# A gated linear recurrence feeding a top-1 expert layer: experts processed in the rank of their counts, with room by rank and shared tiles in quarters

## The chip, the cores and the metric

The kernel runs on one core of one Trainium2 chip. A core has a matrix engine (TensorE, shown as PE for the matmuls and PEld for its loads of the stationary operand), a vector engine (DVE), a scalar engine (ACT), GpSimd (POOL) and SyncE (SP), which here only issues DMAs. All engines run their own instruction streams in order and wait for each other through semaphores. 16 DMA engines move data between HBM and the on-chip memory (SBUF); matmuls write to PSUM, which has eight banks. The metric is the device time of one execution in microseconds.

## The reference

```python
# attention: B, H, S, D = 4, 8, 768, 48
mag = sqrt(a_re**2 + a_im**2); scale = minimum(mag, 0.999) / (mag + 1e-6)
a_re, a_im = a_re * scale, a_im * scale
for t in range(S):                       # complex state (D x D) per batch and head
    new_re = ar * S_re - ai * S_im
    new_im = ar * S_im + ai * S_re
    S_re, S_im = new_re + outer(k[t], v[t]), new_im
    y[t] = q[t] @ S_re
x = y as (3072 tokens, 384)              # B*S tokens, H*D columns
# expert layer: 8 experts, hidden size 1024
logits = x @ w_gate                      # (3072, 8)
e = argmax(logits); gate = softmax(logits)[e]
out[token] = gate * (relu(x[token] @ w1[e]) @ w2[e])     # w1: 384x1024, w2: 1024x384
```

Each token goes to exactly one expert, so how many tokens an expert gets depends on the data. With the given inputs the reference sends 354, 406, 392, 388, 370, 421, 338 and 403 tokens to experts 0 to 7.

## The kernel before

The kernel has two stages, and each has an order of instructions that is written out ahead of time. A class `Plan` collects operations with an engine, an assumed duration, what they read and write, and for DMAs an assumed latency and time on the wire. `Plan.order` tries many list schedules with slightly different priorities (seeded noise) and keeps the one with the shortest planned span; the instructions are then emitted in that order, so every engine's stream is the planner's choice. Changing one operation's assumed duration can change the order of all the others.

**Stage one (plan P)** computes the recurrence by chunks of 128 tokens. `front(u)` turns the gates of one unit (up to 384 tokens of one batch) into scaled q and k with ACT, DVE and POOL and moves them by DMA (`hz<-zp`) into a layout for matmuls. `chunk(b, c)` does the matmuls of one chunk: scores (L403), masking on DVE (`am`), outputs (L415, L422), the state (L430), and at the end L438, which turns the result so that tokens lie on partitions and adds the eight logits; ACT copies it into `xg`.

`route(b, r0, r1)` handles several chunks at a time: maximum, softmax sum, one-hot choice, and a place for each token. The place comes from matmuls with a strictly triangular matrix and a matrix of ones (L479 to L484) plus `cumb`, the running counts, which start at `e * CAP`: expert `e` owns rows `e * CAP` to `e * CAP + CAP - 1` of the HBM tensor `xs_hbm`, with `CAP = 448`. POOL then scatters each chunk's 128 rows with one indirect DMA (L498). Each row holds the token's features, its gate weight and its token number. Places from 256 on that no token takes are filled beforehand by three DMAs of 64 rows for each expert from the tile `empty` (L531), with a token number that is out of bounds, so that nothing is written for them later. Batches 0 to 2 are routed once; batch 3 is routed in three parts, chunks 0 to 2, 3 to 4 and 5.

**Between the stages** a few DVE operations and two matmuls (L560, L570) check that the fast way is valid, among other things that every expert's count lies between 256 and `CAP`. If not, the flag `again` sends the program into a slow loop that recomputes everything.

**Stage two (plan M)** processes experts 0 to 7 in order. `weights(e)` loads w1 (L611) and w2 (L613) of expert `e`, 1.5 MB each, into one of three buffers; for experts 0 and 1 that happens before anything else of the plan. `tokens(e, s)` fetches the expert's 448 rows with four DMAs (`xb<-xs_hbm`, L620; for expert 0 two of the four go through the ACT queue), and the gate weights and token numbers (`gi`, `hg`). DVE transposes the rows in 32x32 blocks (L632) into `xrt`. Then:

- L647, first product: 8 hidden parts of 128 by 3 steps over the features, each a matmul with 448 moving columns. DVE (L650) and ACT (L653) take turns at the relu into `ht`.
- L661, second product: for the first 384 tokens, three output tiles of 128 tokens; each is 8 matmuls with 384 moving columns (the w2 columns), the tokens being the stationary operand.
- L673, shared tiles: the remaining 64 places of two neighbouring experts share one output tile, one expert at partitions 0 to 63, the other at 64 to 127. Each of the 8 steps is two matmuls with 64 stationary columns and 384 moving columns.
- `finish`: DVE multiplies with the gate weight into one of four `yo` buffers (L605), and POOL scatters the 128 rows to the output by token number (L594).

All matmuls here are fp32, and each shows as two MATMUL records in the trace, with a LDWEIGHTS record each. So 24 matmuls of one expert's first product are 48 records.

Of the kernel before, what the change touches and what calls it, by code (L numbers as in the profile page):

```python
# [30 lines left out]
CAP = 448  # L31
# [3 lines left out]
NB = CAP // 32  # L35
# [129 lines left out]
def gateloop_then_moe(ctx, tc, gates, qk, v, wg, w1, w2, out):  # L165
# [50 lines left out]
    ones_b = const([128, 128], "ones_b", 1.0, BF16)  # L216
    cum = const([128, E], "cum")
# [7 lines left out]
    with ExitStack() as att:  # L225
# [278 lines left out]

        def setup():
# [14 lines left out]
        with tc.manual_schedule():  # L520
            for u in range(NU):
# [7 lines left out]
                if u == 3:  # L529
                    for h in range(3):  # L530
                        P.add("SP", 0.65, lambda h=h: nc.sync.dma_start(  # L531
                            xs_hbm.rearrange("(e s) w -> s e w", e=E)[MINC + 64 * h:MINC + 64 * h + 64],
                            bc(empty[0:64, None, :], [64, E, W])), (), (("empty", h),), lat=2, wire=3.2, after=moved[1])
                for c in range(t0 // 128, t1 // 128):
                    chunk(b, c, t1 - t0 == TU)
                    for r0, r1 in ROUTES[b]:
                        if r1 == c + 1:
                            route(b, r0, r1)
            for i in P.order():
# [25 lines left out]
    nc.vector.tensor_scalar(out=f4, in0=f4, scalar1=float(CAP), scalar2=None, op0=ALU.is_le)  # L565
# [8 lines left out]
    with ExitStack() as ms:  # L574
# [4 lines left out]
        NW = 3  # L579
        w1b = buf("w1b", NW, [128, DT * F])  # L580
        w2b = buf("w2b", NW, [128, FT * DM])
        xrt = buf("xrt", 2, [128, DT, CAP])
        ht = buf("ht", 2, [128, FT, CAP])
        yo = buf("yo", 4, [128, DM])
        hg = buf("hg", 2, [128, 2])
        xb = buf("xb", 2, [128, NB, 96])
        gi = buf("gi", 2, [128, 3, 2])
        HB, OB = bank[0:5], bank[5:8]
        M = Plan()
# [12 lines left out]
        def finish(ob, gate, index, reads):  # L602
            yi = cnt["y"] % 4
# [5 lines left out]
        def weights(e):  # L609
            ws = e % NW  # L610
            M.add("SP", 0.65, lambda: nc.sync.dma_start(w1b[ws], w1[e * 128:e * 128 + 128, :]), (), (("w1", ws),), lat=1.9, wire=5.2,  # L611
                  after=rows[-1:])
            M.add("SP", 0.65, lambda: nc.sync.dma_start(w2b[ws], w2[e * 128:e * 128 + 128, :]), (), (("w2", ws),), lat=1.9, wire=5.2,  # L613
                  after=rows[-1:])

        def tokens(e, s):

            for i in range(4):
                eng, dma = ("ACT", nc.scalar) if e == 0 and i % 2 else ("SP", nc.sync)
                j = M.add(eng, 0.65, lambda i=i, dma=dma: dma.dma_start(  # L620
                    xb[s][32 * i:32 * i + 32], xs_hbm[e * CAP:(e + 1) * CAP, 104 * i:104 * i + 96].rearrange("(j p) w -> p j w", p=32)),
                    ("routed",), (("xb", s, i),), lat=2.5 if e == 0 else 6.0, wire=0.9)
            if e:
                rows.append(j)
            z, hgi = e % 2, e // 2 % 2
            M.add("SP", 0.65, lambda: nc.sync.dma_start(
                gi[s], xs_hbm[e * CAP:e * CAP + 384, XW:W].rearrange("(j p) w -> p j w", p=128)), ("routed",), (("gi", s),), lat=3.0, wire=0.5)
            M.add("SP", 0.65, lambda: nc.sync.dma_start(
                hg[hgi][64 * z:64 * z + 64], xs_hbm[e * CAP + 384:(e + 1) * CAP, XW:W]), ("routed",), (("hg", hgi, z),), lat=3.0, wire=0.1)
            for j in range(4):  # L630
                b0, b1 = 4 * j, min(4 * j + 4, NB)
                M.add("DVE", (b1 - b0) * 96 * 0.00105 + 0.1, lambda b0=b0, b1=b1: nc.vector.transpose(  # L632
                    xrt[s][:, :, 32 * b0:32 * b1].rearrange("p d (b t) -> p b d t", t=32),
                    xb[s][:, b0:b1].rearrange("p b (d c) -> p b d c", d=DT)), tuple(("xb", s, i) for i in range(4)), (("xrt", s, j),))

        def expert(e):
            s, ws = e % 2, e % NW
            if e > 1:
                weights(e)
            tokens(e, s)  # L640
# [204 lines left out]
```

## Time and profile before

| | |
|---|---|
| median of 6 runs | 565.81 us (564.5 to 569.49) |
| the profiled execution | 566.71 us, of which 565.0 us are its span |
| mean granted TensorE clock | 0.934 |
| busy in the span | PE 479.2, PEld 322.7, DVE 269.2, ACT 201.6, POOL 112.0 us |
| stage one ends with the matmuls of the check | 257.73 us |
| first matmul of stage two | 267.22 us |
| last shared tile starts | 554.53 us |
| first product, 384 records | 150.9 us busy |
| second product, 384 records | 128.4 us busy |
| shared tiles, 128 records | 21.5 us busy |

A record's own duration is longer than its share of the time, because matmuls overlap in the pipeline: what a matmul costs in a row of them is the distance from one start to the next. The numbers of lines are those of the kernel before.

### The profile page before, as it was taken

Reading aid. Unit: us, or ns where it says so; the run is one execution under the profiler, and the core shown is the slowest. Engines: PE = TensorE matmul, PEld = TensorE weight load, DVE = VectorE, ACT = ScalarE, POOL = GpSimd, SP = SyncE. Lnnn points to the kernel's source line nnn. Section 1 sums busy time; section 2 is a strip of 40 time slices with the busy share of each in tenths; the row PEclk is TensorE's granted clock in tenths of the full one; section 3 lists DMA queues with packets and bytes.
Section 4 is the critical chain, followed back from the end, with each engine's and each line's share of the span. In section 5 each row is a group of like instructions: output and inputs, shape, how many; then the busy total and the mean of one; then the engine's idle time right before and its main releaser. Section 6 shows DMA issues by size and latency. Waiting matters only on the chain. (4 is left out here: it accounts for less than half of the span.)

```text
span 565.0 us, 6970 instructions
## 1 busy us (share of the span) xinstructions
PE 479.2 (85%) x2689; PEld 322.7 (57%) x2689; DVE 269.2 (48%) x429; ACT 201.6 (36%) x289; POOL 112.0 (20%) x116
## 2 busy tenths in 40 slices
PE   0065797976988999971999999999999999999996
PEld 0055696865877989860455545555455554555552
DVE  6899989798999997333212021022011120110111
ACT  6896788888687676220100000100000000000100
POOL 6253113044512510430001001010011010100202
PEclk9996779696998899995899999999999999999999
DMA  8767666659999873876926063067343300400101
GB/s 266 206 209 201 162 215 177 203 155 293 289 243 224 258 177 106 329 293 119 280 37 174 15 172 139 13 237 181 52 149 127 112 29 0 139 14 0 34 24 48
DMA packets 48425, 86.15 MB, mean 152 GB/s; under 512 B 22513, under 2 KB 37905, under 8 KB 46337
## 3 DMA queue, kind: packets, MB, share of 16 engines
q1 hardware_dynamic: 43840, 75.19, 47.2%
q0 software_dynamic: 3328, 9.86, 4.7%
q10 hardware_dynamic: 1216, 0.59, 0.5%
q8 instruction: 23, 0.38, 0.3%
q14 instruction: 18, 0.14, 0.1%
HBM read 54.32 MB, written 13.21 MB: 120 GB/s over the span
## 5 line engine op out<-in xcount | busy, mean ns | idle before, releaser
L647 PE MATMUL bank<-xrt,w1b 128*128 128x448 f32 x384 | 150.9, 546 | 9.3 <-DVE xrt L632 9.3
L661 PE MATMUL bank<-w2b,ht 128*128 128x384 f32 x384 | 128.4, 487 | 0.0
L647 PEld LDWEIGHTS bank<-xrt,w1b 128*128 128x128 f32 x384 | 74.0, 193 | 79.2 <-issue 63.4
L653 ACT ACTIVATE ht<-bank 128x448 f32<-128x448 f32 x32 | 17.4, 544 | 254.6 <-PE bank L647 229.6
L661 PEld LDWEIGHTS bank<-w2b,ht 128*128 128x128 f32 x384 | 72.7, 190 | 54.3 <-issue 10.3
L403 PE MATMUL bank<-hz 128*128 128x128 f32 x384 | 61.4, 313 | 36.4 <-DMA hz<-zp 35.4
L403 PEld LDWEIGHTS bank<-hz 128*128 128x128 f32 x384 | 54.6, 221 | 40.4 <-issue 32.6
L594 POOL DMA_INDIRECT out_dram<-yo,gi x24 | 23.5, 980 | 271.1 <-DVE yo L605 245.8
L650 DVE TENSOR_SCALAR ht<-bank 128x448 f32<-128x448 f32 x32 | 20.0, 624 | 95.2 <-PE bank L647 90.9
L605 DVE TENSOR_SCALAR yo<-bank,gi 128x384 f32<-128x384 f32 x24 | 14.8, 617 | 96.6 <-PE bank L661 91.8
L422 PE MATMUL bank<-am,v 128*48 128x128 f32 x384 | 30.3, 292 | 19.9 <-DVE am L178 19.6
L178 DVE TENSOR_TENSOR zp<-Z,cs 128x1152 f32<-128x1152 f32 (+2 forms) x40 | 44.5, 1151 | 3.6 <-ACT cs L267 1.5
L178 POOL TENSOR_TENSOR AB<-AB,C 128x1152 f32<-128x1152 f32 (+2 forms) x9 | 22.3, 2478 | 81.7 <-ACT C L267 81.7
L498 POOL DMA_INDIRECT xs_hbm<-xg,slot x24 | 26.8, 1115 | 51.0 <-issue 16.0
L438 PE MATMUL bank<-turn,yt 128*128 128x104 f32 x192 | 30.7, 308 | 7.1 <-ACT yt L426 5.6
L322 DVE TENSOR_TENSOR_SCAN D<-AB,lend,C 128x384 f32<-128x384 f32 (+2 forms) x30 | 36.6, 1269 | 0.3
L422 PEld LDWEIGHTS bank<-am,v 128*48 128x48 f32 x384 | 20.9, 129 | 24.7 <-DVE am L178 22.4
L178 DVE TENSOR_TENSOR am<-bank,causal 128x512 f32<-128x512 f32 x48 | 31.7, 678 | 5.5 <-PE bank L403 5.5
L430 PE MATMUL bank<-v,kt 128*96 128x48 f32 x320 | 33.9, 263 | 0.3 <-ACT kt L398 0.3
L430 PEld LDWEIGHTS bank<-v,kt 128*96 128x96 f32 x320 | 32.3, 181 | 2.7 <-issue 1.7
L632 DVE STREAM_TRANSPOSE xrt<-xb 128x384 f32<-128x384 f32 (+1 forms) x32 | 14.0, 496 | 40.0 <-PE bank L647 32.6
L438 PEld LDWEIGHTS bank<-turn,yt 128*128 128x128 f32 x192 | 27.1, 216 | 9.2 <-ACT yt L426 6.1
(110 smaller groups left out, 477.8 us busy)
## 6 DMA issues: line engine op xcount, KB each, us to landing
w1b<-in_w_dram SPq DMA_DIRECT2D x8, 1536.0 KB
w2b<-in_w_dram SPq DMA_DIRECT2D x8, 1536.0 KB
hz<-zp SPq DMA_DIRECT2D x24, 432.0 KB
AB<-in_gates_dram SPq DMA_DIRECT2D x12, 576.0 KB
Z<-in_qk_dram SPq DMA_DIRECT2D x12, 576.0 KB
xb<-xs_hbm SPq DMA_DIRECT2D x30, 168.0 KB
v<-in_v_dram SPq DMA_DIRECT2D x8, 576.0 KB
xs_hbm<-empty SPq DMA_DIRECT2D x3, 836.0 KB
```

The costliest lines, as they stand in the source:

```text
L178: (eng or nc.vector).tensor_tensor(out=o, in0=a, in1=b, op=op)
L322: P.add("DVE", 2 * T * 0.00105 + 0.19, lambda g=g: nc.vector.tensor_tensor_scan(d[:, g, :], a[:, g, :], c[:, g, :], lend[:, b, g, c0:c0 + ...
L403: nc.tensor.matmul(SC[hf][:, (h % 4) * 128:(h % 4) * 128 + 128], lhsT=hk[:, h], rhs=hq[:, h], start=True, stop=True)
L422: nc.tensor.matmul(YT[ps, (h // 2) * 128:(h // 2) * 128 + 128], lhsT=V[:, cl, h * D:h * D + D], rhs=am[2 * par + hf][:, h % 4, :], start=( ...
L430: nc.tensor.matmul(ST[0:96, h * D:h * D + D], lhsT=kt[par][:, h * 96:h * 96 + 96], rhs=V[:, cl, h * D:h * D + D], start=(c == 0 and h == 0 ...
L438: nc.tensor.matmul(XT[:, p * 104:p * 104 + 104], lhsT=yt[par][:, p * 128:p * 128 + 128], rhs=turn[:, p, :], start=True, stop=True)
L498: i = nc.gpsimd.indirect_dma_start(out=xs_hbm[:, :], out_offset=bass.IndirectOffsetOnAxis(ap=R[slot][:, c:c + 1], axis=0), in_=xg[:, (g0 + ...
L594: i = nc.gpsimd.indirect_dma_start(out=out[:, :], out_offset=bass.IndirectOffsetOnAxis(ap=index, axis=0), in_=y, in_offset=None, bounds_ch ...
L647: nc.tensor.matmul(HB[hb][:, 0:CAP], lhsT=w1b[ws][:, c:c + 128], rhs=xrt[s][:, d, :], start=(d == 0), stop=(d == DT - 1))
L650: M.add("DVE", 0.6, lambda f_=f_, hb=hb: nc.vector.tensor_scalar_max(ht[s][:, f_, :], HB[hb][:, 0:CAP], 0.0), (("H", hb),), (("ht", s, f_),))
L653: M.add("ACT", 0.6, lambda f_=f_, hb=hb: nc.scalar.activation(ht[s][:, f_, :], HB[hb][:, 0:CAP], func=ACT.Relu), (("H", hb),), (("ht", s, ...
L661: nc.tensor.matmul(OB[ob][:, 0:DM], lhsT=ht[s][:, f_, j * 128:j * 128 + 128], rhs=w2b[ws][:, f_ * DM:f_ * DM + DM], start=(f_ == 0), stop= ...
```

## The change

1. **Room by rank.** `CAP` becomes 480 places in HBM for each expert, but the number of places that are computed depends on the rank of the expert's count: `CAPS`. The ranks are found on the chip by `ranks()`, from the counts after 21 of the 24 chunks (after the route of chunks 0 to 2 of batch 3): one matmul and six small DVE operations write `order`, the expert of each rank.
2. **Order of experts by rank.** Stage two runs over turns 0 to 7; turn `e` takes the expert of rank `TURNS[e]`. Its number is read into a register on SP (for turn 0 on ACT as well), and weights, rows, gate weights and token numbers are fetched from addresses that the register gives. All of these loads now have to wait for `order`. Only the weights of turn 0 are ahead of the first rows; before, it was two experts' weights.
3. **Shared tiles by 32.** Three experts share one output tile in quarters of 32 rows, twice: places 384 to 479 of turn 0 and 384 to 415 of turn 1 in one tile, places 384 to 447 of turn 2 and 384 to 415 of turns 3 and 4 in another. Turns 5 to 7 have 384 places and no rest. To keep what they need, there are four w2 buffers and three `ht` buffers instead of three and two.
4. **Fill** of the places from 256 on in parts of 64, 64 and 96 rows for each expert, instead of three times 64.
5. **Eight output buffers** `yo` instead of four.
6. **The check** compares the final counts, taken by rank, with `CAPS`.

```diff
-CAP = 448
+CAP = 480
+CAPS = (480, 448, 416, 416, 416, 384, 384, 384)
+TURNS = (0, 2, 1, 3, 4, 5, 6, 7)
+SHARED = ((1, ((0, 384, 0), (0, 416, 32), (0, 448, 64), (1, 384, 96))), (4, ((2, 384, 0), (2, 416, 32), (3, 384, 64), (4, 384, 96))))
...
+        def ranks():
+            cnt = bank[2][:, 440:440 + E]
+            P.add("PE", 0.3, lambda: nc.tensor.matmul(cnt, lhsT=ones_b, rhs=cumb, start=True, stop=True), ("cumb",), ("RT",))
+            def dv(fn, r, w):
+                P.add("DVE", 0.2, fn, r, w)
+            full = [128, E, E]
+            dv(lambda: tt(key, cnt, keyb, ALU.subtract), ("RT",), ("key",))
+            dv(lambda: tt(tmp, bc(key[:, None, :], full), bc(key[:, :, None], full), ALU.is_le), ("key",), ("tmp",))
+            dv(lambda: nc.vector.tensor_reduce(above, tmp, axis=AX, op=ALU.add), ("tmp",), ("above",))
+            dv(lambda: tt(pick, bc(above[:, None, :], full), bc(rev[:, :, None], full), ALU.is_equal), ("above",), ("pick",))
+            dv(lambda: tt(tmp, pick, bc(e_f[:, None, :], full), ALU.mult), ("pick", "above"), ("tmp",))
+            def f():
+                    nc.vector.tensor_reduce(order, tmp, axis=AX, op=ALU.add)
+            dv(f, ("tmp",), ("order",))
+            P.add("", 14.0, lambda: None, ("order",), ("prefetch",))
...
                     for h in range(3):
-                            xs_hbm.rearrange("(e s) w -> s e w", e=E)[MINC + 64 * h:MINC + 64 * h + 64],
-                            bc(empty[0:64, None, :], [64, E, W])), (), (("empty", h),), lat=2, wire=3.2, after=moved[1])
+                        h0, h1 = MINC + 64 * h, (MINC + 64, MINC + 128, CAP)[h]
+                            xs_hbm.rearrange("(e s) w -> s e w", e=E)[h0:h1],
+                            bc(empty[0:h1 - h0, None, :], [h1 - h0, E, W])), (), (("empty", h),), lat=2, wire=3.7, after=moved[1])
...
                         if r1 == c + 1:
                             route(b, r0, r1)
+                            if b == B - 1 and r1 == 3:
+                                ranks()
...
-    nc.vector.tensor_scalar(out=f4, in0=f4, scalar1=float(CAP), scalar2=None, op0=ALU.is_le)
+    tt(tmp, pick, bc(f4[:, None, :], [128, E, E]), ALU.mult)
+    nc.vector.tensor_reduce(f4, tmp, axis=AX, op=ALU.add)
+    tt(f4, f4, caps, ALU.is_le)
...
-        NW = 3
+        NW, NV, NH = 3, 4, 3
-        w2b = buf("w2b", NW, [128, FT * DM])
+        w2b = buf("w2b", NV, [128, FT * DM])
-        ht = buf("ht", 2, [128, FT, CAP])
-        yo = buf("yo", 4, [128, DM])
+        ht = buf("ht", NH, [128, FT, CAP])
+        yo = buf("yo", 8, [128, DM])
...
         def weights(e):
+            def f():
+                which[e] = ds(nc.values_load(order[0:1, TURNS[e]:TURNS[e] + 1], engines=ENG[0:2 if e == 0 else 1], min_val=0, max_val=E - 1,
+                                             skip_runtime_bounds_check_because="experts have numbers below E"), 1)
+            M.add("SP", 0.3, f, (), (("which", e),), after=rows[-1:])
+            for wb, wv, nb, nm in ((w1b, w1v, NW, "w1"), (w2b, w2v, NV, "w2")):
+                first = M.add("SP", 0.65, lambda wb=wb, wv=wv, nb=nb: nc.sync.dma_start(wb[e % nb][:, None, :], wv[:, which[e], :]),
+                              (("which", e),), ((nm, e % nb),), lat=1.9, wire=5.2, after=rows[-1:] if nm == "w1" else [first])
...
-                    xb[s][32 * i:32 * i + 32], xs_hbm[e * CAP:(e + 1) * CAP, 104 * i:104 * i + 96].rearrange("(j p) w -> p j w", p=32)),
+                    xb[s][32 * i:32 * i + 32, None, 0:nb, :], xv[:, which[e], 0:nb, 104 * i:104 * i + 96]),
...
-                        nc.tensor.matmul(HB[hb][:, 0:CAP], lhsT=w1b[ws][:, c:c + 128], rhs=xrt[s][:, d, :], start=(d == 0), stop=(d == DT - 1))
+                        nc.tensor.matmul(HB[hb][:, 0:n], lhsT=w1b[e % NW][:, c:c + 128], rhs=xrt[s][:, d, 0:n], start=(d == 0), stop=(d == DT - 1))
...
-                        for z in range(2):
-                            nc.tensor.matmul(OB[ob][64 * z:64 * z + 64, 0:DM], lhsT=ht[z][:, f_, 384:CAP],
-                                             rhs=w2b[(e - 1 + z) % NW][:, f_ * DM:f_ * DM + DM], start=(f_ == 0), stop=(f_ == FT - 1),
-                                             skip_group_check=True)
+                            for t, m, c0, p0 in parts:
+                                nc.tensor.matmul(OB[ob][p0:p0 + m, 0:DM], lhsT=ht[t % NH][:, f_, c0:c0 + m],
+                                                 rhs=w2b[t % NV][:, f_ * DM:f_ * DM + DM], start=(f_ == 0), stop=(f_ == FT - 1),
+                                                 skip_group_check=len(parts) > 1)
...
             weights(0)
-            weights(1)
```

## The prediction

> **What bounds the kernel now.** I read the chain of what ended last first; it holds only four pieces, the last 1.1 us, so it does not say what sets the span. Next the page's slices of 14.1 us:
>
> ```profile
> PE   0065797976988999971999999999999999999996
> DVE  6899989798999997333212021022011120110111
> PEclk9996779696998899995899999999999999999999
> ```
>
> DVE leads up to slice 15, then come a few slices of mixed work, one slice in which PE is nearly empty, and from there PE alone. The windows put numbers on it (the columns are the stretch, its length, the busy time of PE, PEld, DVE, ACT and POOL, PE's clock, the DMA share and GB/s):
>
> ```profile
> 120.00:180.00 60.00, 50.35 (x519) 45.06 (x518) 58.03 (x70) 47.41 (x68) 21.25 (x14) 0.91 0.94 250
> 225.00:258.00 33.00, 24.38 (x267) 21.51 (x265) 11.35 (x58) 8.30 (x19) 12.40 (x15) 0.90 0.70 271
> 258.00:267.00 9.00, 0.00 (x0) 0.00 (x0) 1.69 (x5) 0.00 (x0) 0.01 (x1) 0.50 0.74 150
> 333.00:360.00 27.00, 27.00 (x94) 13.57 (x93) 3.73 (x6) 1.63 (x3) 1.96 (x2) 1.00 0.34 97
> 450.00:500.00 50.00, 50.00 (x162) 26.60 (x161) 8.64 (x16) 2.18 (x4) 4.89 (x5) 1.00 0.15 54
> ```
>
> From 267 us PE never stops; DMA and the other engines are far from full. So stage two lasts as long as its matmuls, and every matmul slot removed there is time gained, as long as nothing else makes PE wait. The price of a slot comes from PE's timeline (start, length, then the group):
>
> ```profile
> 267.22 20.73 PE L647 MATMUL bank<-xrt,w1b 128*128 128x448 f32 x48 [9.31 <-DVE xrt L632]
> 333.65 5.38 PE L673 MATMUL bank<-w2b,ht 128*64 128x384 f32 x32
> 338.96 2.85 PE L661 MATMUL bank<-w2b,ht 128*128 128x384 f32 x8
> 414.52 13.69 PE L647 MATMUL bank<-xrt,w1b 128*128 128x448 f32 x36
> 428.05 2.74 PE L661 MATMUL bank<-w2b,ht 128*128 128x384 f32 x8
> 528.96 13.06 PE L661 MATMUL bank<-w2b,ht 128*128 128x384 f32 x40
> 541.86 2.42 PE L647 MATMUL bank<-xrt,w1b 128*128 128x448 f32 x6
> ```
>
> Start to next start: 13.53 us for 36 records is 0.3758 us for 448 columns; 12.90 for 40 is 0.3225 for 384 columns. Between them lie 0.0533 us for 64 columns, 0.00083 a column. A shared tile, 32 records, takes 5.31 us: 16 pairs of 0.3225 are 5.16, and 0.15 goes at its two edges. So two matmuls of 64 stationary columns, side by side in the array, cost one slot. Check: 384 x 0.3758 + 384 x 0.3225 + 4 x 5.31 = 289.4; the first seven records run at half clock and cost 2.5 more; 291.9 of the 292.7 us from 267.22 to the end of the last shared tile (554.53 + 5.38 = 559.91).
>
> **The change part by part.**
>
> *First product.* The places computed are 480 + 448 + 3 x 416 + 3 x 384 = 3328 instead of 3584, 48 records a turn. Slots: 0.4024, 0.3758, 0.3491 and 0.3225 us for 480, 448, 416 and 384 columns. Sum 48 x (0.4024 + 0.3758 + 3 x 0.3491 + 3 x 0.3225) = 134.1 instead of 144.3: **-10.2 us**. The full tiles of the second product stay at 384 records.
>
> *Shared tiles.* Two tiles instead of four, each of 16 steps, but four matmuls of 32 stationary columns in a step (128 records, as before). No row shows four side by side. Lower bound of a step: one slot, 0.3225. Upper bound: four in a row, 1.29. The nearest row is the pair above, same operands and moving columns, where the second matmul adds nothing to the step; and the loads do not stand in its way:
>
> ```profile
> 334.03 0.14 PEld L673 LDWEIGHTS bank<-w2b,ht 128*64 128x64 f32 x2 [0.18 <-issue]
> ```
>
> Both loads of a pair are over in 0.14 us, under the matmuls before them. I take 0.3225. In the changed kernel's listing of PE, one of the two tiles is cut in halves with other work between, so there are three blocks with edges: 32 x 0.3225 + 3 x 0.15 = 10.8 instead of 21.2: **-10.4 us**; with the upper bound it would be +20.6.
>
> The Trainium skill, "TensorE: Matmul & The Clock Gate", section "Part 3: Packing small matmuls — row/col tiling", speaks against this: it says that a weight load runs beside matmuls in flight only if it goes to other rows of the array, and here all four use all 128 rows. The row above has such loads fully beside matmuls, so I keep the row. The same section gives 2.38x, not 3x, for three column tiles; an estimate from it for four, at the same efficiency, is a step of 0.41 us, 2.7 us more in all, and the sum would end at 549.
>
> *Waits in stage two.* Weights come later: before, those of two experts were issued at 227.4 us:
>
> ```profile
> 227.41 0.82 SPq L611 DMA_DIRECT2D w1b<-in_w_dram  x2
> 228.33 1.26 SPq L613 DMA_DIRECT2D w2b<-in_w_dram  x2
> 259.87 6.20 SPq L620 DMA_DIRECT2D xb<-xs_hbm  x6
> ```
>
> Now SP first waits for `order`. In the listing, some 68 matmuls stand on PE between that of the ranks and that of the final count (L560, at 256.3 us); by the rows of their kinds (1.08 us for 8 of L415 or L422, 1.5 for 8 of L430, about 1.1 for 4 of L403 or L438) that is 13 us, so the ranks' matmul is at about 243 and `order` 2 us later (six DVE operations 0.2 us apart and one mask of 0.7). Reading a register from SBUF took 0.48 us on SP (the row of L688). A weight block of 1.57 MB takes 5.3 us at the 297 GB/s that the stretch 268 to 280 moved; the two of turn 0 land at about 252 and 257, twice as slow at 257 and 267. The first is needed at 267.2, the second at 286.7 (after 42 records of 480 columns and the slow clock). Cost 0; without that cover, `order` at the very end would cost about 2 us. SP has nothing of stage one queued behind this wait. ACT's register read stands behind the last softmax operation and ends before the last rows land.
>
> The weights of turn 1 are issued after seven of the eight row fetches of turns 0 and 1, and the eighth is queued behind them: rows until about 267, 3.15 MB at 297 GB/s until 278, the last rows and four transposes (0.5 us each) until 283. PE's listing wants them after 42 records of turn 0 and half a tile, at 267.2 + 19.4 + 2.6 = 289. Bounds 0 and, if the fetches take twice as long, 5 us; I take 0, the slack being 6. Later loads have a whole turn of some 34 us each; SP's further register reads and address instructions are hidden by its waits for PE (90.5 us for buffers of w2 alone).
>
> *Before the first matmul.* Turn 0 fetches and transposes 15 blocks of 32 rows instead of 14: 1/14 of the 5.5 us from 259.9 to 265.4 is 0.4, at most, since the other fetches share it; transposes +0.1. **+0.4**. The idle 9.3 us remain, and so does the slow clock after them.
>
> *Stage one.* The fill grows by 32 x 8 rows of 1672 bytes, 0.43 MB; at 307 GB/s (stretch 153 to 160) that is 1.4 us of full DMA. PE waited for DMA in only four places between 30 and 250 us, 7.3 us in all: bounds 0 and 1.4, **+0.4**. The ranks' six DVE operations, 1.2 us, fall into 225 to 258, where DVE is busy a third of the time; 0 to 1.2, **+0.2**. The check's two more DVE operations lie under the landing of rows. The listing shows that the order differs on all five engines in stage one. What that does I can only bound: PE waited 19.6 us in eight places for masks (longest 7.9), 2.5 each; one such wait more or less is 2.5 either way, and I take 0.
>
> *Eight output buffers.* DVE waited 13.1 us for scatters to release `yo`, but PE did not wait for DVE: 0.
>
> **Sum:** -10.2 - 10.4 + 0.4 + 0.4 + 0.2 = -19.6. The profiled execution (565.0 span, 1.7 around it, 566.7) becomes 547.1; it lies 0.9 above the median, so **546.2 us**.
>
> **Rivals.**
> (a) *Quarters run two at a time*: 32 steps x 0.3225 more, +10.3, 556.5. For it: only pairs have been seen. Against: nothing in the pair's step shows a resource at its limit.
> (b) *Quarters run one after the other*: +31.0, 577, **slower than before**. The side changes when a step costs 0.3225 + 19.6 / 32 = 0.94 us, close to three slots. Against it speaks the pair's row.
> (c) *A new wait of PE for weights or rows in the first turns*: 2 to 8 us (half to all of a late 3 MB load), 548 to 554. For it: in the first 30 us of stage two 3.15 MB more are to be moved than before, with 297 GB/s already used from 268 to 280. Against: the slack of 6 us above.
> (d) *Stage one's new order is worse or better* by more than 2.5: worse to 552, better to 541.
> (e) *The change does not do what it says*: counts above `CAPS` would start the slow loop. By the reference, the counts in the order of the ranks after 21 chunks are 421, 406, 403, 392, 388, 370, 354, 338, below 480, 448, 416, 416, 416, 384, 384, 384. PE's work does not depend on how the ranks come out, since the sizes belong to the turns. I give it less than 1 in 100.
>
> **How the numbers follow.** Forecast case 0.70 (own range 543 to 550, from the bounds of fill, ranks and order), (a) 0.07, (b) 0.03, (c) 0.12, (d) 0.07, (e) and unknown losses 0.01. 540 to 555 leaves out (a), (b), (e) and the ends of (c) and (d), about 0.15. Half a per cent, 2.8 us, is about what this kernel's measurement can tell from no change. Slower by more: (b), (e) and the far end of (d), 0.05; within: 0.02; faster: 0.93.
>
> **What the profile after would show.** Right: first-product records at distances of 0.40 to 0.32 us, 3328/3584 of the time; two shared tiles of about 5.3 us, loads of 32 columns in fours; first weight DMA near 246 and landed before the last rows; PE full from about 267 to 540. Wrong: steps of 0.65 or 1.29 us in the shared tiles; PE idle in the first 40 us of stage two with `w1b` or `xrt` as releaser; the first matmul of stage two more than 3 us away from 267.6, for stage one.

## The result, and the profile after

The changed kernel takes 551.91 us (median of 20 runs, 547.12 to 555.88), the kernel before 566.43 us beside it (46 runs, 563.58 to 571.02): ratio 0.9733, 95% interval 0.9712 to 0.9754. That is 14.5 us less; 19.6 less were forecast. One of the six executions of run 7 below, 592.40 us at a granted clock of 0.83, is left out of that run's ratio. The profiled execution of the changed kernel took 551.72 us, span 550.0. Between the two profiled executions the 15.0 us lie here:

| stretch, us | before | after | difference | forecast |
|---|---|---|---|---|
| start to the check's last matmul (L570, L610) | 257.73 | 261.85 | +4.1 | +0.6 |
| from there to the first matmul of stage two | 9.49 | 10.60 | +1.1 | +0.4 |
| from there to the end of the last tile | 292.7 | 272.3 | -20.4 | -20.6 |
| rest of the span | 5.1 | 5.3 | +0.2 | 0 |

So stage two did what was worked out for it, and nearly all of the 4.6 us that are missing were lost before it.

The page's slices of the changed kernel, 13.75 us each:

```profile
PE   0046869298988989976199999999999999999996
DVE  6989989999999899624102320011311111111011
PEclk9997679687988979978589999999999999999999
```

From the 21st slice on PE is full, as before. The 18th (234 to 247 us) is new: PE at 7 tenths and its clock at 7, late in stage one. The 20th is the stand ahead of stage two.

The windows that answer to those shown of before (same columns; stage two starts 5 us later, hence 258 to 272):

```profile
225.00:258.00 33.00, 26.54 (x287) 24.38 (x286) 10.70 (x48) 10.18 (x21) 11.48 (x14) 0.89 0.52 189
258.00:272.00 14.00, 0.55 (x5) 0.22 (x4) 4.26 (x24) 0.16 (x1) 0.99 (x1) 0.50 0.66 118
333.00:360.00 27.00, 27.00 (x104) 14.20 (x103) 3.10 (x5) 1.63 (x3) 3.02 (x4) 1.00 0.05 17
450.00:500.00 50.00, 50.00 (x156) 29.45 (x155) 8.40 (x15) 3.44 (x7) 4.70 (x5) 1.00 0.13 42
```

PE is again the only full engine from the first product on. Its timeline in stage two:

```profile
272.45 19.96 PE L701 MATMUL bank<-xrt,w1b 128*128 128x480 f32 x42 [10.41 <-DVE xrt L686]
...
333.99 2.42 PE L701 MATMUL bank<-xrt,w1b 128*128 128x448 f32 x6
336.34 2.79 PE L720 MATMUL bank<-w2b,ht 128*32 128x384 f32 x32
339.05 2.52 PE L701 MATMUL bank<-xrt,w1b 128*128 128x448 f32 x6
...
394.30 8.54 PE L701 MATMUL bank<-xrt,w1b 128*128 128x416 f32 x24
402.68 5.32 PE L720 MATMUL bank<-w2b,ht 128*128 128x384 f32 x16
...
430.08 15.98 PE L720 MATMUL bank<-w2b,ht 128*128 128x384 f32 x96
445.90 7.90 PE L701 MATMUL bank<-xrt,w1b 128*128 128x384 f32 x24
```

The line at 336.34 is half of a shared tile: 8 steps of four matmuls with 32 stationary columns. From its start to the next start are 2.71 us. Eight slots of 0.3225 are 2.58; 0.13 go at the edges. So a step of four costs one slot. The other half takes 2.72 us (361.17 to 363.89), and the second shared tile, 64 of the 96 records of the line at 430.08, takes 5.29 us (437.92 to 443.21). From 394.30 to 402.68 are 24 records of 416 columns, 0.349 us each, as worked out from the 0.00083 us of a column. The loads of the four quarters lie under the matmuls, as those of the pairs did:

```profile
336.69 0.13 PEld L720 LDWEIGHTS bank<-w2b,ht 128*32 128x32 f32 x4 [0.19 <-issue]
```

Where the 4 us of stage one went shows in PE's timeline near 232 us. The changed kernel:

```profile
232.54 0.19 PE L497 MATMUL bank<-oh,ones_b 128*128 128x16 bf16 x2
236.87 1.74 PE L428 MATMUL bank<-hz,sb 128*48 128x128 f32 x16 [4.15 <-issue]
238.55 2.80 PE L443 MATMUL bank<-v,kt 128*96 128x48 f32 x16
241.27 1.95 PE L435 MATMUL bank<-am,v 128*48 128x128 f32 x16
243.15 1.53 PE L416 MATMUL bank<-hz 128*128 128x128 f32 x8
244.52 0.17 PE L520 MATMUL bank<-cumb,ones_b 128*128 128x8 bf16 x1
```

PE stands for 4.15 us and then works at about half pace (granted clock 0.51 from 237.1 to 244.0): the L443 group takes 2.80 us where other groups of 16 take 1.48, the L435 group 1.95 where others take 1.04. It cannot issue L428 because ACT has not yet written `sb`, and ACT waits for the L443 group of 229.89, which PE had finished at 231.37. The trace also records when a semaphore is counted up: PE's count for that group came at 236.32, 4.95 us later. The counts for the matmuls behind it (L416, L494, L497, done by 232.7) came at 237.8 to 237.9. ACT and DVE start as soon as the counts are there (`remote` stands where the profile finds nothing that ended just before):

```profile
236.35 0.47 ACT L447 COPY sb<-bank 96x384 f32<-96x384 f32 x1 [4.17 <-remote]
237.83 0.69 DVE L181 TENSOR_TENSOR am<-bank,causal 128x512 f32<-128x512 f32 x1 [5.23 <-remote]
```

POOL was issuing six row scatters (L511) from 228.77 to 236.23, 0.3 us apart. The kernel before has such late counts too, at the same scatters of batch 2 (232.17 to 236.14, 3.97 us), but PE had other work in its queue:

```profile
232.10 0.96 PE L422 MATMUL bank<-am,v 128*48 128x128 f32 x13
233.23 0.42 PE L422 MATMUL bank<-am,v 128*48 128x128 f32 x3 [0.17 <-issue]
233.58 0.61 PE L438 MATMUL bank<-turn,yt 128*128 128x104 f32 x3
234.66 0.69 PE L438 MATMUL bank<-turn,yt 128*128 128x104 f32 x4 [0.47 <-issue]
236.07 0.25 PE L438 MATMUL bank<-turn,yt 128*128 128x104 f32 x1 [0.72 <-issue]
```

There the gaps add up to 1.4 us and no slow stretch follows. That was the reading to be tested: is it the new order by itself (theory A), or the new order together with signals that the scatters hold up (theory S)?

SP's queue shows the loads that now depend on `order`:

```profile
247.58 0.38 SPq L662 DMA_DIRECT2D w1b<-in_w_dram  x1
248.16 0.35 SPq L662 DMA_DIRECT2D w2b<-in_w_dram  x1
264.25 2.23 SPq L670 DMA_DIRECT2D xb<-xs_hbm  x4
```

The weights of turn 0 leave 3 us after the ranks' matmul (244.52), 17 us ahead of the first row fetch. With 295 and 419 GB/s moved from 248 to 252 and 252 to 256, their 3.1 MB are down by about 257 (an estimate), before the last rows are scattered.

### The profile page after: what moved, and what is told of

It is laid out like the page before. It is cut to its first block, busy times and chain, and to the rows that moved or that the text cites. A ratio compares the mean times of both kernels' runs of the same rounds, so it can differ in the third digit from the quotient of the medians.

```text
span 550.0 us, 7115 instructions
## 1 busy us (share of the span) xinstructions
PE 457.9 (83%) x2690; PEld 321.1 (58%) x2690; DVE 269.6 (49%) x432; ACT 201.3 (37%) x289; POOL 114.2 (21%) x125
## 5 line engine op out<-in xcount | busy, mean ns | idle before, releaser
L701 PE MATMUL bank<-xrt,w1b 128*128 128x416 f32 (+3 forms) x384 | 141.3, 521 | 10.4 <-DVE xrt L686 10.4
L720 PE MATMUL bank<-w2b,ht 128*128 128x384 f32 (+1 forms) x512 | 138.7, 487 | 0.0
L720 PEld LDWEIGHTS bank<-w2b,ht 128*128 128x128 f32 (+1 forms) x512 | 76.7, 170 | 59.1 <-issue 11.6
L707 ACT ACTIVATE ht<-bank 128x416 f32<-128x416 f32 (+3 forms) x32 | 16.6, 518 | 255.1 <-PE bank L701 248.4
L416 PE MATMUL bank<-hz 128*128 128x128 f32 x384 | 63.6, 323 | 37.6 <-DVE zp L181 34.6
L416 PEld LDWEIGHTS bank<-hz 128*128 128x128 f32 x384 | 57.7, 233 | 40.5 <-DVE zp L181 34.6
L704 DVE TENSOR_SCALAR ht<-bank 128x416 f32<-128x416 f32 (+3 forms) x32 | 18.9, 591 | 114.2 <-PE bank L701 109.0
L181 DVE TENSOR_TENSOR zp<-Z,cs 128x1152 f32<-128x1152 f32 (+2 forms) x40 | 48.6, 1251 | 0.6 <-ACT cs L280 0.3
L435 PE MATMUL bank<-am,v 128*48 128x128 f32 x384 | 30.0, 299 | 10.5 <-DVE am L181 10.4
L511 POOL DMA_INDIRECT xs_hbm<-xg,slot x24 | 27.7, 1154 | 48.3 <-DVE slot L504 26.2
L443 PE MATMUL bank<-v,kt 128*96 128x48 f32 x320 | 35.5, 271 | 2.4 <-ACT kt L411 2.4
L443 PEld LDWEIGHTS bank<-v,kt 128*96 128x96 f32 x320 | 34.2, 189 | 3.6 <-ACT kt L411 2.9
L181 POOL TENSOR_TENSOR Z<-Z,AB 128x1152 f32<-128x1152 f32 (+2 forms) x9 | 22.2, 2468 | 48.1 <-ACT AB L280 42.6
L335 DVE TENSOR_TENSOR_SCAN D<-AB,lend,C 128x384 f32<-128x384 f32 (+2 forms) x30 | 31.1, 1073 | 0.3
```

The lines of the kernel that those rows point to most:

```text
L181: (eng or nc.vector).tensor_tensor(out=o, in0=a, in1=b, op=op)
L335: P.add("DVE", 2 * T * 0.00105 + 0.19, lambda g=g: nc.vector.tensor_tensor_scan(d[:, g, :], a[:, g, :], c[:, g, :], lend[:, b, g, c0:c0 + ...
L416: nc.tensor.matmul(SC[hf][:, (h % 4) * 128:(h % 4) * 128 + 128], lhsT=hk[:, h], rhs=hq[:, h], start=True, stop=True)
L435: nc.tensor.matmul(YT[ps, (h // 2) * 128:(h // 2) * 128 + 128], lhsT=V[:, cl, h * D:h * D + D], rhs=am[2 * par + hf][:, h % 4, :], start=( ...
L443: nc.tensor.matmul(ST[0:96, h * D:h * D + D], lhsT=kt[par][:, h * 96:h * 96 + 96], rhs=V[:, cl, h * D:h * D + D], start=(c == 0 and h == 0 ...
L511: i = nc.gpsimd.indirect_dma_start(out=xs_hbm[:, :], out_offset=bass.IndirectOffsetOnAxis(ap=R[slot][:, c:c + 1], axis=0), in_=xg[:, (g0 + ...
```

## The experiments

They ran in three sets; within a set the kernels ran on one chip, beside the same runs of the kernel before: 561.40 us in the first (1 to 4), 568.60 in the second (5 to 8), 565.94 in the third (9 to 12). The first and the third set ran on the same chip. "Late" below is the delay, in the kernel's profiled execution, of the count of the state's matmuls near 230 us (L443 above, L430 in the kernel before), the one that ACT's `sb` waits for. In none of the four traces of the first set was a count late by more than 0.6 us, there or elsewhere.

**1. The changed kernel with stage one in the order of before.** The planner is given stage one as it was; the ranks' matmul and its DVE operations are hung on behind.

```diff
...
-            P.add("PE", 0.3, lambda: nc.tensor.matmul(cnt, lhsT=ones_b, rhs=cumb, ...), ("cumb",), ("RT",))
+            hooks[P.cumb] = [lambda: nc.tensor.matmul(cnt, lhsT=ones_b, rhs=cumb, ...)]   # after cumb of chunks 18 to 20
...
-                P.add("DVE", 0.2, fn, r, w)
+                late.append(fn)                                                            # after the last mask
...
-            P.add("", 14.0, lambda: None, ("order",), ("prefetch",))
...
-  ... lat=2, wire=3.7, after=moved[1])
+  ... lat=2, wire=3.2, after=moved[1])
...
```

> The changed kernel, with stage one in the order of the kernel before; the ranks' matmul and six DVE operations are appended behind the running counts and behind the last mask. Theory A (the 4 to 5 us that stage two starts later come from stage one's new order): first matmul of stage two at 267 to 269 us, time 545 to 548. Rival B (they come from the loads that wait for the order of experts, or from the register reads, whatever stage one's order): start at 271 or later, time 551 or more; B should even gain here, as the order is known later.

548.09 us (545.73 to 549.68), ratio 0.9767 (0.9737 to 0.9797): 4.5 us slower than the changed kernel itself in the same set (run 4). The check's last matmul starts at 250.96, 1.9 us earlier than there (252.85), and the last row scatter ends at 250.88, but the row fetch is issued only at 258.71. PE's line says for what:

```profile
267.08 8.13 PE L709 MATMUL bank<-xrt,w1b 128*128 128x480 f32 x15 [15.93 <-DMA xb<-xs_hbm]
```

With this order `order` is known later, the weights of turn 0 are issued at 245.92 instead of 238.91, and 3.1 MB are on the wire just when the last rows are to land (425 GB/s from 252 to 256). So the new order, with its early `order`, is worth more here than the 1.9 us that it costs. The numbers of theory A (a start at 267 to 269, 545 to 548 us) are nearly met, but not for its reason: in this set the changed kernel itself starts stage two at 263.53. That the weights on the wire hold up the row fetch is so far read from two things that happen at the same time; run 6 tests it.

**2. The kernel before with stage one of the changed kernel.** The ranks are computed and not used.

```diff
...
+    e_f, keyb, key, above, pick, tmp, order = ...      # as in the changed kernel
...
+        def ranks(): ...                               # as in the changed kernel
...
-  ... lat=2, wire=3.2, after=moved[1])
+  ... lat=2, wire=3.7, after=moved[1])
...
+                            if b == B - 1 and r1 == 3:
+                                ranks()
```

> The kernel before, with the changed kernel's stage one: the ranks are computed but not used, and the fill is planned as long as in the changed kernel, so PE, DVE and ACT have the changed kernel's order up to the check. Fixed room, experts in order, weights of two experts loaded early, as before. Theory A: stage two starts at 271 to 272, time 570 to 571.5, 0.7 to 0.9% slower than before. Rival B: start at 267 to 268, time 566 to 567.

563.27 us, ratio 1.0022 (1.0001 to 1.0043), 1.9 us by the medians. Without late counts the new order costs 1 to 2 us, so theory A, that it costs the 4 us by itself, falls. Its trace has a wait at the last route that the kernel before does not have: `slot` has two buffers, and DVE waits for a scatter that still reads the older one. The trace is of the slowest of the twelve executions (567.80 us; the others 560.91 to 564.66), and the same wait is 0.67 us in run 4, so how much of the 1.9 us it makes is not shown.

```profile
257.32 0.16 DVE L501 TENSOR_REDUCE slot<-z 128x1 int32<-128x8 f32 x1 [4.08 <-DMA xs_hbm<-xg,slot]
```

**3. The changed kernel with the scatters of batch 2 held back** until the counts of chunks 18 to 20 are known.

```diff
+                if b == 2:
+                    held.append(f)
+                    f = lambda: None
...
+                if i == P.cumb:                       # after cumb of chunks 18 to 20
+                    nc.gpsimd.tensor_copy(seen, cumb)
+                    for fn in held:
+                        fn()
```

> The changed kernel; the six scatters of batch 2 wait, by a small POOL copy in front of them, until the running counts of chunks 18 to 20 are written. The other engines' order is unchanged. Theory S (the burst of scatters holds up the signals of PE, so PE, ACT and DVE stand still from 231.4 to 236.3 and PE goes on at half clock): the stand at that place is gone, the ranks' matmul comes at 238 to 240 instead of 244.5, stage two starts at 267 to 269 and the time is 547 to 549, if the burst does not hold up something as important later. Rival O (the order alone makes PE wait for ACT there): the stand of 4 us stays between the same operations, time 551 to 553.

544.14 us (541.44 to 546.65), ratio 0.9693 (0.9653 to 0.9732), against 0.9689 of run 4: the same. It says nothing on theory S, since nothing was late in this set.

**4. The changed kernel unchanged.** No edit.

> The changed kernel once more, to see whether its stand near 232 to 237 us is there in every execution. If it belongs to the order: a stand of 4 to 5 us of PE between the matmuls of the third-to-last route and the next L428, start of stage two at 271 to 273, time 550 to 553. If it was a chance of one execution: no such stand, start at 267 to 269 and a time that still has a median near 552 would then need another cause.

543.61 us (542.48 to 545.60), ratio 0.9689 (0.9661 to 0.9718): 17.8 us less than before, not 14.5. Neither branch of the expectation fits: there is no stand, and stage two starts at 263.53, earlier than either had it. Where the first trace had 4.15 us of idle time and slow groups, this one has

```profile
231.00 0.19 PE L497 MATMUL bank<-oh,ones_b 128*128 128x16 bf16 x2
231.12 1.08 PE L428 MATMUL bank<-hz,sb 128*48 128x128 f32 x16
232.13 1.56 PE L443 MATMUL bank<-v,kt 128*96 128x48 f32 x16
233.62 1.08 PE L435 MATMUL bank<-am,v 128*48 128x128 f32 x16
234.63 1.16 PE L416 MATMUL bank<-hz 128*128 128x128 f32 x8
235.62 0.17 PE L520 MATMUL bank<-cumb,ones_b 128*128 128x8 bf16 x1
```

From L497 to the ranks' matmul are 4.6 us, in the first trace 12.0. Stage two takes 271.9 us here.

**5. The kernel before with its shared tiles in quarters**, and nothing else.

```diff
-                            nc.tensor.matmul(OB[ob][64 * z:64 * z + 64, 0:DM], lhsT=ht[z][:, f_, 384:CAP],
-                                             rhs=w2b[(e - 1 + z) % NW][:, f_ * DM:f_ * DM + DM], ...)
+                            for q in (64 * z, 64 * z + 32):
+                                nc.tensor.matmul(OB[ob][q:q + 32, 0:DM], lhsT=ht[z][:, f_, 384 + q % 64:416 + q % 64],
+                                                 rhs=w2b[(e - 1 + z) % NW][:, f_ * DM:f_ * DM + DM], ...)
```

> The kernel before, with its four shared tiles cut into quarters: each of the 16 pairs of 64 stationary columns becomes four matmuls of 32 columns, 64 more steps of matmuls in all and nothing else. My theory (four matmuls side by side in the array cost one slot, as in the changed kernel's trace): a shared tile stays at 5.3 us and the time is within 1 us of before. Rival, quarters run two at a time and the changed kernel's gain came from elsewhere: each tile takes 10.5 us, the time is 20.6 us above before.

566.86 us, ratio 0.9972 (0.9948 to 0.9996): no slower; the 1.7 us less are a little more than the expected 1 us, and no run explains them. The timeline's line for a shared tile of this kernel:

```profile
336.80 5.37 PE L674 MATMUL bank<-w2b,ht 128*32 128x384 f32 x64
```

64 records in 5.37 us, where before it was 32 records in 5.38. Rivals (a) and (b) of the prediction are excluded by this alone.

**6. Run 1 with w2 of turn 0 behind the row fetches of turn 0.**

```diff
... (the edit of run 1)
-            for i in M.order():
+            todo = M.order()
+            w2_0 = loads[1]                             # loads: the weight loads in order
+            todo.remove(w2_0)
+            fetch = [i for i, o in enumerate(M.ops) if o["name"].startswith("('xb', 0,")][:4]
+            todo.insert(max(todo.index(i) for i in fetch) + 1, w2_0)
+            for i in todo:
...
```

> The changed kernel with stage one in the order of before (as in the first run), and now the w2 weights of turn 0 are issued behind the four row fetches of turn 0; w1 stays ahead of them. Theory (in the first run the 3.1 MB of weights, issued at 246 us, lay on the wire while the last rows were being scattered, so that the row fetch started 7.8 us after the last scatter instead of 2.4): the row fetch follows the last scatter by 2 to 4 us and the time falls by about 4 us, to 0.968 to 0.970 of before. Rival (the gap belongs to the order of stage one, not to the wire): no change, 0.977.

553.35 us (551.53 to 555.36), ratio 0.9725 (0.9693 to 0.9757); this misses the expected 0.968 to 0.970 and can't be told from run 1. In the trace the expected thing happened, but not only that: the row fetch follows the last scatter by 2.4 us instead of 7.8, then it takes longer.

```profile
265.00 0.87 SPq L679 DMA_DIRECT2D xb<-xs_hbm  x2
266.06 0.36 SPq L670 DMA_DIRECT2D w2b<-in_w_dram  x1
266.95 0.86 SPq L679 DMA_DIRECT2D xb<-xs_hbm  x2
```

The 1.57 MB of w2 now share the wire with the rows: from the first fetch to the first transpose are 8.6 us instead of 6.4 in run 4. From the end of the last scatter to the first product it is 16.2 us in run 1, 12.9 here and 10.7 in run 4, where the weights are down before. This execution also had late counts (4.1 us near 232 us, 4.3 at 251 us), which run 1 had not, so the total times of the two are not to be compared. That the gap is gone speaks for the wire as its cause, but does not show it alone: here w1 was also issued 10.1 us ahead of the end of the last scatter, in run 1 both loads 5.0 us ahead. What holds is that neither place for w2 brings the first product as soon after the last scatter as an early `order` does.

**7. The changed kernel with idle matmuls** in the 10 us in which PE stands ahead of stage two.

```diff
...
             for i in M.order():
                 M.ops[i]["fn"]()
+                if i == loads[0]:                    # the load of w1 of turn 0
+                    for _ in range(9):
+                        nc.tensor.matmul(OB[1][:, 0:512], lhsT=w1b[0][:, 0:128], rhs=w1b[0][:, 0:512], start=True, stop=True)
```

> The changed kernel with nine idle matmuls of 512 columns between the check and the first product of turn 0, into a PSUM bank that nobody reads then, so that PE does not stand for 10 us before stage two. If the standing is what leaves the first matmuls of stage two at half clock: they run at full clock, and the time falls by about 2.5 us against the changed kernel (0.965 where that is 0.969). Rival 1: the clock falls anyway in the short gap that is left, no change. Rival 2: the idle matmuls end after the first rows are ready, 0 to 1 us longer.

548.89 us, ratio 0.9641 (0.9606 to 0.9676). The changed kernel did not run in this set, so the total is not set against it; the gain is read from the timeline:

```profile
261.83 10.26 PE L742 MATMUL bank<-w1b 128*128 128x512 f32 x18
272.38 17.17 PE L702 MATMUL bank<-xrt,w1b 128*128 128x480 f32 x42 [0.28 <-DVE xrt L687]
```

The 42 records take 17.17 us instead of 19.96, and stage two 269.5 us instead of 272.3: 2.8 us. The windows of the changed kernel's first trace and of this run (clock: the last column but two) say the same:

```profile
272.00:300.00 28.00, 27.55 (x65) 13.55 (x66) 5.20 (x10) 2.23 (x4) 0.00 (x0) 0.89 0.89 275
272.00:300.00 28.00, 27.72 (x75) 13.98 (x75) 5.13 (x10) 2.75 (x5) 0.00 (x0) 1.00 0.96 276
```

The standing is what makes the first matmuls slow. The Trainium skill, "TensorE: Matmul & The Clock Gate", section "Part 1: The HAM clock gate (the "warmup" mystery)", has the array at half clock after standing, until it has been busy for about 3.4 us. The direction is that of these lines, the length is not: in the changed kernel the granted clock is 0.5 from 272.45 to 278.1, 5.6 us of work, and here it is 0.5 for the first 4.6 us of the idle matmuls (261.8 to 266.4) and 1 from there on.

**8. The changed kernel with four output buffers.** PE's order is the same.

```diff
-        yo = buf("yo", 8, [128, DM])
+        yo = buf("yo", 4, [128, DM])
-            yi = cnt["y"] % 8
+            yi = cnt["y"] % 4
```

> The changed kernel with four output buffers instead of eight; PE's order is the same in both. The prediction put the eight buffers at nothing: same time as the changed kernel within 1 us. Rival (DVE, held by the scatters, now holds up the relu and with it PE): 1 to 5 us longer, and PE has idle time in stage two. Also to be seen: whether the stand of 4 us that PE had near 232 us in the changed kernel's first trace comes again in this trace, since stage one is the same.

560.52 us (556.01 to 560.95), ratio 0.9839 (0.9803 to 0.9874): 5.5 to 6.0 us more than the changed kernel's 0.9733 and 0.9742 in sets that also had late counts (here by 3.6 us), and more than the rival's 1 to 5. Stage two takes 279.7 us instead of 272.3, and PE's and DVE's timelines show why:

```profile
447.54 5.97 PE L701 MATMUL bank<-xrt,w1b 128*128 128x384 f32 x18
457.91 4.21 PE L701 MATMUL bank<-xrt,w1b 128*128 128x384 f32 x6 [4.41 <-DVE ht L704]
461.91 3.70 PE L720 MATMUL bank<-w2b,ht 128*128 128x384 f32 x8
```

```profile
447.74 0.62 DVE L651 TENSOR_SCALAR yo<-bank,gi 128x384 f32<-128x384 f32 x1 [9.57 <-PE bank L720]
456.78 0.62 DVE L651 TENSOR_SCALAR yo<-bank,hg 128x384 f32<-128x384 f32 x1 [8.42 <-DMA out_dram<-yo,gi]
457.31 1.01 DVE L704 TENSOR_SCALAR ht<-bank 128x384 f32<-128x384 f32 x2
```

DVE waits 8.4 us for the scatter that still reads the `yo` buffer that it wants for the second shared tile, and two relus stand behind it in DVE's order. PE waits 4.4 us for a relu to free a PSUM bank and then loses another 3 at half pace. DVE's order is not quite that of the changed kernel: with four buffers the planner puts the second shared tile's multiply behind another output tile's, not ahead of it. The prediction put the eight buffers at nothing; with the order that the planner makes for four, they are worth 7.4 us.

**9. The changed kernel once more.** No edit.

> The changed kernel unchanged, to stand beside the next three on the same chip. Stage two 272 us. If PE's signals arrive late during the burst of six scatters near 230 us, as in the first trace, PE stands 3 to 4 us there and the ratio to before is about 0.973; if no signal is late, as in the four traces of the first runs, about 0.969.

550.91 us (549.41 to 553.88), ratio 0.9742 (0.9700 to 0.9785). A count is late by 4.93 us, and PE stands as in the first trace:

```profile
234.61 1.95 PE L428 MATMUL bank<-hz,sb 128*48 128x128 f32 x16 [4.13 <-issue]
236.48 2.80 PE L443 MATMUL bank<-v,kt 128*96 128x48 f32 x16
```

The chip is that of run 4. So it is not the chip that decides whether counts are late; what does was not found.

**10. Run 2 once more.** The edit is that of run 2.

> The kernel before with stage one of the changed kernel, once more. Theory: the new order costs 1 to 2 us by itself (1.9 measured) and some 2 to 3 more where PE's signals are late, since the ranks' matmul and the route then leave PE nothing else to do: 1.005 to 1.008 in such a case, 1.002 without. Rival: the new order costs the same 1 to 2 us whether signals are late or not, 1.002 to 1.004.

569.90 us, ratio 1.0063 (1.0032 to 1.0094), a count late by 6.34 us, PE standing 5.5 us near 231 us. With late counts the new order costs 3.6 to 4.0 us, without them 1.2 to 1.9 (run 2; the two intervals overlap a little). The value lies in the range that theory S gave and above the rival's 1.002 to 1.004, though the interval reaches down into that; the stand in the trace is what speaks against the rival.

**11. The changed kernel with a memset of about 1 us on POOL between the scatters of batch 2.**

```diff
+        rest = const([128, 1024], "rest")
...
+                    if b == 2 and c < n - 1:
+                        nc.gpsimd.memset(rest, 0.0)
                 P.add("POOL", 1.27, f, ...)
```

> The changed kernel with a memset of about 1 us on POOL between the six scatters of batch 2, so that they no longer follow each other at 0.3 us. Theory (signals are held while scatters are issued back to back): no signal of PE is later than 1.5 us near 230 us, PE does not stand there, and the time is 1 to 3 us below the changed kernel where that one shows the stand, the same where it does not. Rival (each scatter holds signals for itself, or the delay is of another cause): still late by 2 us and more, the time the same or up to 3 us longer, since the rows of batch 3 are scattered later.

544.10 us (541.34 to 547.00), ratio 0.9608 (0.9555 to 0.9662): 6.8 us less than run 9 on the same chip, more than the 1 to 3 us expected. No count near 230 us is later than 1.28 us, and PE goes on:

```profile
230.25 0.19 PE L498 MATMUL bank<-oh,ones_b 128*128 128x16 bf16 x2
230.37 1.08 PE L429 MATMUL bank<-hz,sb 128*48 128x128 f32 x16
231.38 1.56 PE L444 MATMUL bank<-v,kt 128*96 128x48 f32 x16
```

From the L497/L498 group to the ranks' matmul are 4.6 us instead of 12.7 in run 9: 4 us of standing and 4 at half pace, of which only the first had been reckoned with. Some of that is given back later (the check ends 6.3 us earlier, not 8.1): at the last route DVE waits 1.68 us for a scatter to release `slot`, the wait that run 2 showed as well.

**12. Run 11 with the idle matmuls of run 7.**

> The one before with the nine idle matmuls ahead of stage two as well: 2.5 to 3 us less than it, by the start of stage two at full clock (stage two 269.4 instead of 272.3 us, as measured). Rival: that the earlier run gained by its chip, no difference.

544.19 us (543.10 to 545.63), ratio 0.9611 (0.9569 to 0.9653): by the times no gain. Its stage two took 269.5 us instead of 271.6 in run 11, but its profiled execution was already 2.4 us behind at the route near 227 us, long before the added matmuls. With five times each, spread over 2.5 and 5.7 us, a gain of 2 us can't be told from none; whether both edits add up stays open. Run 11 is faster than the kernel before and the changed one; that run 12 is better still is not shown.

## Why the prediction was right, and where it was off

The sign and the range were right (546.2, 540 to 555; measured 551.9). The value was 5.7 us too low, and outside the forecast case's own range of 543 to 550. What came was rival (d), to which the prediction gave 0.07 ("worse to 552"); the stated range holds the result because it had room for (c) and (d).

- *First product, -10.2.* Right. Stage two as a whole is 20.4 us shorter, by slots of 0.349 us for 416 columns and 0.3225 for 384, as in the step; the slow start took 5.6 us instead of 4.9 in the kernel before, which costs 0.4 us.
- *Shared tiles, -10.4.* Right. A step of four quarters costs a slot, and the three blocks take 2.71 + 2.72 + 5.29 = 10.7 us with their edges, where 10.8 were worked out; run 5 shows it in the other kernel. The rule that the prediction cited from the Trainium skill ("TensorE: Matmul & The Clock Gate", "Part 3: Packing small matmuls — row/col tiling") did not hold here: the loads use all rows and ran beside the matmuls (0.13 us for four at 336.69). The estimate made from that section, 0.41 us a step, was 0.07 us above the 0.339 us that the block at 336.34 measures with its edges.
- *Waits in stage two, 0.* Right: the first weight DMA was issued at 247.6, and PE had no idle time from 272.45 to the end. That the ranks' matmul stood at 244.5 where 243 was worked out is partly luck: it stands 15.5 us ahead of the final count, not 13, but all of that lies 4 us later than before. That the loads stay hidden hangs on an early `order`: in run 1 the first weight DMA is 5.0 us ahead of the end of the last scatter, in run 4 13.9, and the first product follows that end 5.5 us later than in run 4. The prediction had put an `order` at the very end at about 2 us.
- *Before the first matmul, +0.4.* Measured +1.1. In the trace the row fetch starts 2.5 us after the last scatter instead of 1.9 (SP reads its seven waits one after the other, 0.4 us), the four transposes take 1.86 us instead of 1.76, and two fetches of turn 1 are issued 1.4 us after the first of turn 0, where before it was 3.8; how the rest divides among these was not tested.
- *Stage one: fill +0.4, ranks +0.2, new order 0.* This is the step that failed, by its size: "one such wait more or less is 2.5 either way, and I take 0". The check came 4.1 us later, not 0.6. The step bounded the new order by the mean of the waits for masks in the old one. But the order had taken away what PE could do during the scatters of batch 2, so that a late count, which the trace of before already had (3.97 us), became a stand of 4.15 us and 3 more us lost at half clock. Rival (d) named this place, not this mechanism. Runs 2 and 10 give the order's price as 1.2 to 1.9 and 3.6 to 4.0 us, without and with late counts; run 11 removes the delay and gets 6.8 us back, more than the changed kernel had lost against the forecast. Where no count was late (run 4), the gain was 17.8 of the 19.6 us.
- *Eight output buffers, 0.* The reason was wrong, the sum not: DVE's waits for `yo` cost PE nothing in the old order, as said, but in the new order four buffers cost 7.4 us (run 8). The buffers are one of the conditions under which "waits in stage two, 0" holds.
- *What would show it wrong* named a first matmul of stage two more than 3 us from 267.6: it came at 272.45, and it was stage one.

## What to carry to other kernels

The time of a stage that is bound by matmuls could be worked out here from the distances in the timeline to 0.2 us of 20, also for a form that the trace showed only in part. A new order of instructions is different: don't bound it by the mean wait of the old order, but ask for each late signal that the trace already shows what the waiting engine has left to do in the new order, and what its clock does after the stand. And an edit that looks free by the waits of the kernel before can be what keeps another edit free.

## What the runs showed of the hardware that was not expected

- While POOL issued indirect scatters back to back (six, 0.3 us apart), a count of PE's semaphore arrived 3.6 to 6.3 us late in eight traces; the counts of the matmuls behind it came up to 3.0 us after that one. With a memset of 0.97 us between the scatters the largest delay at this place was 1.3 us, in both traces of such kernels. In the four traces of the first set no count was late, on the same chip on which they were in a later set; the kernel before took 561.4 us in the one and 565.9 in the other. What decides that is open, and spacing the scatters of the kernel before was not tried.
- A stand of PE costs more than itself: 4.15 us were followed by four groups that took 8.0 us instead of 4.9 of the same groups in run 4; the 10 us ahead of stage two cost another 2.8.
- Four fp32 matmuls with 32 stationary columns each, all 128 rows and 384 moving columns take as long as one with 128: 64 records in 5.37 us, where 32 with 64 columns take 5.38 and 16 with 128 take 5.32.
